# Attention and SoLU layer on one core: all four full query tiles of batches 1 to 3 turned through DRAM and VectorE instead of two

## The chip, the cores and the metric

The kernel runs on 1 core of one Trainium2 chip. The metric is device time in microseconds (us) of one launch. Before the change three timed runs took 480.44, 481.09 and 484.1 us, so the median is 481.09. The engines are called by the profile's names: PE (TensorE matmul), PEld (its weight load), DVE (VectorE), ACT (ScalarE), POOL (GpSimd) and SP (SyncE, which here only issues DMAs; its queue is SPq). Buffers in PSUM are called `pd` (two banks) and `pg` (one bank).

## What is computed

Attention over 4 batches, 8 heads, 576 positions and 64 columns a head, with rotary position embedding, is laid out as 2304 rows of 512 and goes through a layer with SoLU and a layer norm:

```python
q_rot, k_rot = (rotate(q), rotate(k))
scores = scale * np.matmul(q_rot, k_rot.transpose(0, 1, 3, 2))
scores = scores - np.max(scores, axis=-1, keepdims=True)
attn = np.exp(scores)
attn = attn / (np.sum(attn, axis=-1, keepdims=True) + 1e-09)
x = (attn @ v)            # 2304 rows of 512
h = x @ w_in              # 512 -> 1024
sm = softmax(h); solu = h * sm
ln = (solu - mean) / np.sqrt(var + 1e-06) * g_ln
out = ln @ w_out          # 1024 -> 512
```

All inputs and the output are float32.

## The kernel before

**Stages.** Two heads make a pair; there are 16 pairs, four to a batch. For each pair `stage` turns q and k by the rotary tables (L350, three VectorE or GpSimd operations for each) and, from pair 4 on, splits them into a high and a low part (`kh`, `kl`, `qh`, `ql`). `attention` then takes the 576 query rows of each head in four full tiles of 128 rows (`pair_tile`, i = 0 to 3, both heads at once) and one packed tile that holds the last 64 rows of both heads (`packed`). For a full tile PE makes the scores (L409), DVE takes the row maximum (`mx`, L389) and ACT writes the exponentials to one of four SBUF buffers `e` (L391).

**Turning.** The product with v needs the exponentials with the keys on the partitions, so each full tile and head (an (i, h), eight for a pair) is turned once; the 64 last columns and the packed tile are always turned by PE. `turn_tile` has two ways for it. By PE: four transposes against the identity `idn` (L449) into a `pg` bank, and one copy by ACT or DVE (L319, L321) out of it into `ET`. By DRAM: SP issues a write of the tile to scratch (`escr<-e`, L468, recorded as L334) and, once that has landed, a read back into the same buffer in another order (`e<-escr`, L469), and DVE turns 32 x 32 blocks from it into `ET` (L470, a STREAM_TRANSPOSE). Which (i, h) take the second way is the list `OFFS[P]`. After that come the products with v (L521), the row sums (L535 to L538, `rs`, `rscr`, `Rb`) and the scaled write to `xT` (L526).

**The dense layer.** When a batch is through attention, its tiles of 128 rows go through `front` (L591, 24 matmuls; maximum L598, exponential L600, product L602, then `uscr<-u`, a write to DRAM) and `back` (`wraw<-uscr`, a read; DVE turns it, L643; high and low parts `lnh`, `lnl`, L319 to L321 and L653; L661, 24 matmuls; L664 and L666 write `o`). They run beside the attention of the next batch. The dense layer of batch 3 has no attention beside it and stands at the end.

**Order.** Nothing is scheduled at run time. The kernel body notes every step with the steps it depends on; `ORDER` is a table of numbers in which the steps are then issued, `FLIP` says which of the steps that may run on either of two engines take the second one, and `BUFS` says which buffer of its pool each use takes. Each engine works through its own steps in that order, and so does SP's one DMA queue.

Of the kernel before, what the change touches and what calls it, by code (L numbers as in the profile page):

```python
# [28 lines left out]
OFFS = [()] * 4 + [((0, 0), (0, 1), (2, 0), (2, 1))] * 12  # L29

ORDER = [
    4, 0, 3, 11, 2, 1, 10, 12, 5, 13, 27, 14, 15, 94, 35, 28, 6, 16, 17, 18, 97, 98, 103, 95, 29, 30, 36,
    96, 31, 104, 105, 106, 7, 32, 99, 100, 37, 38, 39, 40, 107, 114, 115, 127, 128, 101, 102, 110, 111, 116,
    117, 84, 89, 33, 108, 112, 129, 113, 83, 109, 19, 118, 20, 86, 85, 87, 136, 139, 137, 121, 138, 91, 119,
    130, 131, 88, 120, 90, 92, 122, 123, 124, 125, 126, 140, 147, 148, 132, 41, 42, 149, 133, 93, 143, 155,
    178, 59, 34, 156, 144, 145, 146, 157, 158, 152, 154, 181, 153, 182, 150, 151, 134, 135, 179, 180, 159,
    170, 169, 187, 171, 141, 176, 173, 142, 172, 174, 183, 184, 60, 163, 164, 165, 188, 189, 211, 190, 191,
    196, 197, 61, 160, 62, 63, 64, 214, 215, 198, 199, 21, 177, 162, 253, 212, 213, 166, 167, 161, 168, 220,
    257, 223, 194, 195, 256, 224, 8, 9, 425, 51, 200, 221, 222, 231, 258, 22, 23, 201, 192, 193, 261, 202,
    218, 185, 232, 24, 219, 43, 186, 254, 233, 239, 240, 216, 217, 255, 229, 230, 262, 265, 263, 241, 25,  # L40
    26, 343, 242, 225, 243, 226, 227, 205, 206, 228, 342, 52, 264, 53, 54, 55, 207, 44, 208, 65, 45, 267,
    271, 268, 266, 236, 238, 260, 56, 209, 337, 237, 274, 275, 269, 272, 204, 270, 273, 295, 246, 203, 244,
    210, 57, 46, 58, 47, 48, 426, 234, 235, 427, 276, 277, 428, 429, 49, 296, 297, 75, 247, 248, 249, 250,
    298, 251, 50, 76, 278, 279, 282, 245, 283, 252, 430, 299, 77, 67, 68, 284, 285, 304, 315, 78, 79, 80,
    280, 300, 281, 301, 344, 175, 289, 290, 291, 259, 305, 306, 316, 317, 292, 293, 307, 338, 339, 69, 70,
    320, 322, 321, 340, 341, 286, 287, 288, 350, 294, 353, 351, 308, 309, 310, 323, 324, 302, 303, 318, 311,
    352, 71, 349, 319, 72, 73, 74, 312, 354, 359, 362, 360, 325, 326, 313, 314, 355, 356, 66, 363, 357, 654,
    434, 358, 383, 386, 384, 443, 444, 435, 436, 437, 438, 439, 331, 332, 333, 361, 653, 364, 385, 365, 392,
    334, 335, 345, 346, 387, 390, 440, 395, 396, 327, 330, 328, 461, 403, 391, 393, 394, 329, 336, 348, 370,
    371, 372, 373, 397, 398, 445, 446, 452, 447, 374, 448, 375, 366, 376, 81, 661, 368, 441, 648, 369, 367,  # L50
    388, 82, 453, 664, 665, 404, 662, 405, 377, 378, 462, 663, 666, 379, 380, 381, 389, 672, 431, 401, 402,
    649, 669, 650, 659, 382, 500, 406, 667, 407, 432, 501, 673, 674, 502, 503, 408, 410, 655, 411, 409, 412,
    413, 414, 415, 504, 399, 454, 675, 676, 670, 677, 696, 400, 419, 420, 421, 422, 423, 656, 678, 463, 464,
    465, 466, 470, 699, 700, 704, 683, 697, 698, 701, 660, 442, 455, 467, 468, 651, 707, 456, 457, 506, 708,
    709, 684, 710, 507, 685, 686, 347, 469, 471, 740, 668, 416, 505, 472, 473, 474, 711, 475, 681, 682, 671,
    508, 509, 519, 520, 510, 712, 713, 718, 497, 719, 657, 417, 476, 477, 705, 679, 680, 521, 418, 424, 511,
    525, 741, 526, 527, 720, 458, 528, 512, 514, 515, 723, 724, 706, 725, 658, 716, 717, 742, 687, 702, 522,
    449, 516, 726, 523, 727, 728, 479, 652, 478, 524, 529, 729, 721, 714, 715, 538, 513, 530, 753, 756, 757,
    539, 751, 690, 433, 691, 517, 692, 754, 755, 746, 693, 689, 531, 694, 703, 761, 722, 764, 767, 480, 765,
    768, 766, 688, 695, 481, 758, 482, 544, 483, 533, 545, 540, 541, 459, 542, 484, 546, 547, 485, 771, 773,  # L60
    774, 543, 769, 460, 534, 762, 763, 772, 788, 734, 486, 487, 759, 735, 736, 737, 738, 532, 557, 558, 770,
    760, 782, 783, 548, 488, 784, 785, 791, 549, 786, 489, 789, 775, 790, 730, 731, 732, 550, 776, 490, 491,
    492, 792, 493, 733, 494, 739, 495, 496, 450, 451, 551, 799, 800, 796, 777, 563, 564, 565, 802, 745, 747,
    778, 576, 580, 566, 743, 744, 801, 797, 581, 582, 748, 749, 518, 498, 803, 499, 591, 535, 779, 780, 577,
    578, 810, 811, 812, 559, 560, 579, 818, 561, 781, 819, 787, 553, 815, 816, 817, 845, 848, 846, 847, 849,
    813, 752, 814, 583, 584, 585, 594, 586, 587, 798, 595, 598, 833, 793, 794, 588, 837, 838, 839, 840, 795,
    820, 821, 589, 590, 592, 808, 809, 552, 850, 562, 804, 805, 806, 807, 856, 826, 827, 828, 829, 830, 822,
    599, 832, 834, 835, 612, 596, 597, 859, 860, 601, 554, 857, 858, 567, 568, 572, 602, 569, 571, 600, 603,
    593, 536, 537, 613, 824, 851, 825, 823, 831, 609, 853, 867, 843, 925, 842, 604, 605, 606, 607, 854, 608,
    614, 868, 852, 869, 870, 750, 616, 617, 570, 610, 611, 615, 880, 883, 865, 866, 881, 884, 882, 861, 862,  # L70
    863, 836, 891, 864, 902, 855, 874, 875, 876, 892, 893, 894, 888, 895, 555, 556, 841, 903, 937, 904, 905,
    618, 924, 926, 940, 941, 871, 877, 906, 910, 573, 844, 929, 927, 872, 873, 878, 879, 907, 909, 885, 928,
    627, 948, 938, 900, 574, 951, 949, 908, 901, 619, 889, 575, 630, 896, 897, 620, 621, 622, 623, 911, 912,
    939, 890, 634, 952, 930, 631, 886, 887, 942, 931, 932, 972, 973, 936, 913, 950, 898, 899, 974, 632, 975,
    976, 959, 624, 625, 626, 953, 628, 983, 984, 914, 985, 945, 954, 977, 986, 633, 987, 635, 980, 915, 916,
    917, 918, 919, 920, 921, 922, 923, 933, 994, 1214, 960, 961, 962, 637, 1215, 957, 638, 943, 958, 978,
    629, 981, 992, 639, 993, 636, 934, 640, 979, 995, 963, 645, 1217, 955, 1218, 1216, 944, 641, 1207, 642,
    643, 935, 1206, 1208, 982, 946, 1209, 947, 644, 1225, 1226, 956, 966, 1210, 996, 967, 1228, 968, 1229,
    1227, 969, 970, 646, 1249, 965, 964, 971, 1219, 988, 989, 1002, 997, 998, 1016, 1017, 1022, 1220, 1003,
    1250, 1251, 990, 1201, 991, 1222, 1004, 1018, 1019, 1252, 1005, 999, 1000, 1001, 1236, 1232, 1020, 1237,  # L80
    1238, 1221, 1213, 1298, 647, 1254, 1239, 1223, 1224, 1021, 1233, 1023, 1234, 1235, 1253, 1006, 1008,
    1024, 1025, 1026, 1007, 1230, 1202, 1203, 1204, 1257, 1035, 1036, 1260, 1261, 1010, 1011, 1012, 1240,
    1013, 1027, 1028, 1014, 1263, 1271, 1009, 1015, 1262, 1255, 1231, 1256, 1205, 1264, 1306, 1272, 1273,
    1212, 1243, 1244, 1245, 1246, 1247, 1309, 1241, 1310, 1294, 1293, 1295, 1299, 1029, 1300, 1242, 1276,
    1278, 1258, 1296, 1030, 1259, 1111, 1277, 1041, 1037, 1038, 1307, 1308, 1248, 1269, 1270, 1042, 1274,
    1279, 1280, 1043, 1281, 1112, 1113, 1039, 1114, 1040, 1115, 1282, 1116, 1275, 1317, 1265, 1266, 1117,
    1305, 1318, 1391, 1319, 1267, 1044, 1054, 1055, 1314, 1045, 1268, 1031, 1032, 1033, 1118, 1304, 1046,
    1050, 1301, 1302, 1119, 1283, 1047, 1287, 1285, 1311, 1288, 1289, 1386, 1290, 1291, 1049, 1315, 1320,
    1321, 1341, 1344, 1345, 1286, 1284, 1292, 1328, 1034, 1329, 1120, 1121, 1326, 1297, 1327, 1122, 1342,
    1123, 1322, 1343, 1124, 1051, 1323, 1352, 1312, 1125, 1313, 1126, 1316, 1355, 1052, 1053, 1330, 1331,  # L90
    1127, 1060, 1048, 1129, 1324, 1056, 1356, 1359, 1057, 1353, 1354, 1346, 1133, 1360, 1363, 1130, 1211,
    1325, 1335, 1336, 1337, 1338, 1339, 1364, 1365, 1332, 1390, 1392, 1347, 1348, 1333, 1371, 1372, 1334,
    1340, 1398, 1399, 1134, 1135, 1393, 1373, 1397, 1349, 1394, 1058, 1059, 1401, 1368, 1131, 1400, 1061,
    1062, 1132, 1374, 1403, 1375, 1128, 1370, 1369, 1357, 1385, 1387, 1388, 1402, 1358, 1350, 1303, 1396,
    1361, 1362, 1478, 1063, 1064, 1065, 1069, 1066, 1136, 1366, 1367, 1351, 1137, 1138, 1068, 1139, 1070,
# [754 lines left out]
```

## Time and profile before

| | before |
|---|---|
| median of 3 runs | 481.09 us |
| the profiled execution's own time | 482.13 us |
| its span, first to last instruction | 480.3 us |
| PE busy | 452.9 us (94%) |
| DVE busy | 391.0 us (81%) |
| ACT busy | 278.5 us (58%) |
| POOL busy | 175.4 us (37%) |
| DMA engines, mean busy share | 57.2% of 16 engines for SP's queue, 86.74 MB |

A busy share is the time in which the engine had an instruction in work, out of the span. Matmuls overlap, and the ends of matmuls are modelled, so PE at 94% is not PE at its peak: how close one matmul stands behind the other is read from the starts in the timeline. The span and the time differ by 1.8 us, which lies ahead of the first and behind the last instruction.

### The profile page before, as it was taken

The numbers are of one execution on the slowest core, as the hardware profiler recorded it, in microseconds if no ns is written. First come the engines' busy times: TensorE is split into PE (matmuls) and PEld (weight loads), VectorE is DVE, ScalarE is ACT, GpSimd is POOL, SyncE is SP. The second block draws the span as 40 slices with busy tenths as digits, with TensorE's granted clock in tenths as the row PEclk, the third lists the DMA queues.
The fourth block names the chain that finished last, engine by engine and source line by source line (L and its number), as shares of the span: only waits on it lengthen the run. The fifth ranks groups of instructions, "written<-read, shape, count | busy, mean of one in ns | idle before, by whom it ended". The sixth has DMA issues, their size and how long they took to land.

```text
span 480.3 us, 8209 instructions
## 1 busy us (share of the span) xinstructions
PE 452.9 (94%) x2880; PEld 330.7 (69%) x2880; DVE 391.0 (81%) x658; ACT 278.5 (58%) x622; POOL 175.4 (37%) x142
## 2 busy tenths in 40 slices
PE   1989999999999999999999999999999999999986
PEld 1555666777777666767777777686777786778865
DVE  3889999998978896879887888978778788675773
ACT  1677979887755655565745564655655555233323
POOL 1033233248367564153633252534621521011120
PEclk9999999999999999999999999999999999999999
DMA  7456565495665665757567476556756456143341
GB/s 268 164 173 226 174 214 165 130 289 180 196 186 172 222 214 183 268 143 226 195 175 239 138 240 228 151 188 201 212 189 177 151 162 194 51 145 111 127 139 64
DMA packets 63610, 87.27 MB, mean 182 GB/s; under 512 B 6080, under 2 KB 44240, under 8 KB 63568
## 3 DMA queue, kind: packets, MB, share of 16 engines
q1 hardware_dynamic: 63568, 86.74, 57.2%
q8 instruction: 23, 0.38, 0.3%
q14 instruction: 19, 0.16, 0.1%
HBM read 59.90 MB, written 26.81 MB: 181 GB/s over the span
## 4 chain that ended last, share of the span: by engine, by line
PE 69%; DVE 19%; ACT 5%; issue 3%; DMA 2%; POOL 1%; SPq 0%; DVEq 0%; ACTq 0%; POOLq 0%
PE pg L661 16%; PE pd L591 15%; PE pg L521 13%; PE pd L409 12%; PE pg L449 10%; DVE mx L389 4%; PE pd L431 2%; DVE tb L643 2%; DVE ET L470 2%; ACT e L391 1%; DVE ms L598 1%; DVE acc L535 1%; ACT u L600 1%; DMA tabs<-in_tab_dram 1%; ACT ET L319 1%
## 5 line engine op out<-in xcount | busy, mean ns | idle before, releaser
L391 ACT ACTIVATE e<-pd,mx 128x576 f32<-128x576 f32 x144 | 106.3, 741 | 63.5 <-DVE mx L389 50.2
L389 DVE TENSOR_REDUCE mx<-pd 128x1 f32<-128x576 f32 x144 | 103.5, 747 | 13.5 <-PE pd L409 11.7
L449 PE MATMUL pg<-idn,e 128*128 128x128 f32 (+1 forms) x464 | 79.1, 294 | 4.5 <-ACT rs L319 1.3
L449 PEld LDWEIGHTS pg<-idn,e 128*128 128x128 f32 (+1 forms) x464 | 63.8, 196 | 25.1 <-issue 4.7
L521 PE MATMUL pg<-ET,vst 128*64 128x320 f32 (+1 forms) x512 | 70.5, 412 | 1.2 <-ACT ET L319 0.9
L591 PE MATMUL pd<-wih,xh 128*128 128x512 f32 x144 | 61.5, 427 | 0.0
L661 PE MATMUL pg<-woh,lnh 128*128 128x512 f32 x144 | 59.5, 413 | 0.7 <-DVE lnh L321 0.7
L661 PE MATMUL pg<-woh,lnl 128*128 128x512 f32 x144 | 56.5, 392 | 1.0 <-DVE lnl L653 1.0
L591 PE MATMUL pd<-wih,xl 128*128 128x512 f32 x144 | 56.6, 393 | 0.0
L591 PE MATMUL pd<-wil,xh 128*128 128x512 f32 x144 | 56.3, 391 | 0.0
L661 PE MATMUL pg<-wol,lnh 128*128 128x512 f32 x144 | 56.2, 390 | 0.0
L470 DVE STREAM_TRANSPOSE ET<-e 128x512 f32<-128x512 f32 x48 | 53.7, 1134 | 2.4 <-DMA e<-escr 2.4
L319 ACT COPY ET<-pg 128x512 f32<-128x512 f32 x82 | 46.6, 587 | 14.1 <-PE pg L449 13.4
L521 PEld LDWEIGHTS pg<-ET,vst 128*64 128x64 f32 x512 | 34.0, 136 | 26.9 <-issue 3.2
L653 POOL TENSOR_TENSOR lnl<-tb,lnh 128x512 fp32r<-128x512 f32 x22 | 28.3, 1287 | 58.5 <-DVE lnh L321 28.3
L643 DVE STREAM_TRANSPOSE tb<-wraw 128x512 f32<-128x512 f32 x36 | 38.6, 1090 | 0.5 <-DMA wraw<-uscr 0.5
L409 PE MATMUL pd<-kh,qh 64*128 64x288 f32 x192 | 35.9, 343 | 0.3 <-ACT e L391 0.3
L409 PE MATMUL pd<-rotk,rotq 64*128 64x288 f32 x128 | 25.2, 482 | 11.1 <-DVE rotq L350 10.3
L350 POOL TENSOR_TENSOR rawk<-rawk,tabs 128x576 f32<-128x576 f32 x18 | 26.0, 1446 | 20.7 <-DMA rawk<-in_k_t_dram 20.7
L661 PEld LDWEIGHTS pg<-woh,lnh 128*128 128x128 f32 x144 | 27.2, 189 | 8.4 <-issue 1.6
L600 ACT ACTIVATE u<-pd,ms 128x1024 f32<-128x1024 f32 x18 | 20.1, 1117 | 22.0 <-DVE ms L598 15.9
L620 POOL TENSOR_TENSOR ms<-ms,half 128x1 f32<-128x1 f32 x18 | 10.4, 578 | 61.1 <-DVE ms L618 58.2
(101 smaller groups left out, 866.9 us busy)
## 6 DMA issues: line engine op xcount, KB each, us to landing
escr<-e SPq DMA_DIRECT2D x48, 256.0 KB
e<-escr SPq DMA_DIRECT2D x48, 256.0 KB
rawq<-in_q_t_dram SPq DMA_DIRECT2D x16, 576.0 KB
uscr<-u SPq DMA_DIRECT2D x18, 512.0 KB
wraw<-uscr SPq DMA_DIRECT2D x18, 512.0 KB
rawk<-in_k_t_dram SPq DMA_DIRECT2D x15, 576.0 KB
vst<-in_v_t_dram SPq DMA_DIRECT2D x16, 320.0 KB
out_dram<-o SPq DMA_DIRECT2D x18, 256.0 KB
```

Source lines behind the costliest of these rows:

```text
L319: nc.scalar.copy(o, i)
L350: add(*c[0], prio, lambda e: e.tensor_tensor(o, a, b, op=op), r, w, alt=c[1], two=True)
L389: add("dve", 672, t, lambda: nc.vector.tensor_reduce(mx[:, mcol:mcol + 1], buf(us)[:, :, 0:288], axis=AX.XY, op=ALU.max, negate=True), [sk ...
L391: add("act", 720, t, lambda: nc.scalar.activation(e.rearrange("p (z n) -> p z n", z=2), buf(us)[:, :, 0:288], AF.Exp, bias=mx[:, mcol:mcol ...
L409: nc.tensor.matmul(buf(us)[:, z, 0:288], a[rows, c0:c0 + 128], w[rows, 288 * z:288 * z + 288], start=(j == 0), stop=(j == len(terms) - 1))
L449: nc.tensor.transpose(dst, src, idn)
L470: add("dve", 1040, t, lambda: nc.vector.transpose(ET[r][:, h, :, q0:q0 + 128].rearrange("p m (a j) -> p j m a", j=4), e.rearrange("p (j b ...
L521: nc.tensor.matmul(buf(uy)[rows, 0:nq], vv[:, m, h, :], e, start=(m == 0), stop=(m == 4))
L591: nc.tensor.matmul(buf(uh)[:, z, :], a[:, c, :], w[:, c, HF * z:HF * z + HF], start=(c == 0 and j == 0), stop=(c == KC - 1 and j == 2))
L643: add("dve", 1050, tl, lambda z=z, turned=turned: nc.vector.transpose(turned().rearrange("p m (a j) -> p j m a", j=4), v[:, :, 128 * z:128 ...
L653: add(*c[0], tl, lambda e, hd=hd, ld=ld, turned=turned: e.tensor_tensor(ld, turned(), hd, op=ALU.subtract), [bk] + kl[0][z], kl[1][z], use ...
L661: nc.tensor.matmul(buf(uo), a[:, f, :], w[:, f, :], start=(f == 0 and j == 0), stop=(f == FC - 1 and j == 2))
```

## The change

`OFFS` lists all eight (i, h) for the pairs 4 to 15 where it listed the four of tiles 0 and 2. Batch 0 (pairs 0 to 3) still turns all of them by PE. With that, `ORDER`, `FLIP` and `BUFS` are other tables: there are 48 steps more (2303) and 48 uses of a buffer fewer.

```diff
-OFFS = [()] * 4 + [((0, 0), (0, 1), (2, 0), (2, 1))] * 12
+OFFS = [()] * 4 + [tuple((i, h) for i in range(4) for h in range(2))] * 12
 
 ORDER = [
...
-    4, 0, 3, 11, 2, 1, 10, 12, 5, 13, 27, 14, 15, 94, 35, 28, 6, 16, 17, 18, 97, 98, 103, 95, 29, 30, 36,
...
 FLIP = {
-    16, 34, 42, 57, 58, 73, 85, 86, 88, 89, 117, 169, 171, 172, 173, 253, 254, 255, 258, 285, 338, 339, 342,
...
+    10, 16, 17, 18, 42, 50, 58, 82, 85, 86, 88, 89, 90, 153, 158, 170, 172, 173, 174, 201, 217, 219, 254,
...
```

What this does to the engines' queues, counted over the whole of both orders: PE has 192 transposes (L449) fewer. SP has 48 writes `escr<-e` and 48 reads `e<-escr` more. DVE has 48 STREAM_TRANSPOSE (L470) more; of other work it has 10 copies `ET<-pg`, 8 casts to `lnh`, 8 subtractions for `lnl`, 4 products for `rawk`, 5 for `rawq` and 3 sums for `rotk` fewer, 2 `xh`, 2 `xl` and 4 weight casts fewer, and some half a dozen small ones either way. ACT has 38 copies `ET<-pg` fewer and 15 casts more. POOL has 13 operations more, among them the 8 for `lnl`, 9 products for `rawk` and `rawq` and 3 sums for `rotk`.

Three places show it. The first is PE in batch 2, between the packed tiles of two pairs (`wih`, `wil` are the parts of the first weights, `xh`, `xl` those of the rows). Before:

```order
L591 MATMUL pd_117<-wih,xl 128x512
L449 MATMUL pg_118<-idn,e_89 128x128 x4
L591 MATMUL pd_117<-wih,xh 128x512
L591 MATMUL pd_117<-wil,xh 128x512
L591 MATMUL pd_117<-wih,xl 128x512
L449 MATMUL pg_119<-idn,e_87 128x128 x4
L591 MATMUL pd_117<-wih,xh 128x512
```

Of the change, the same stretch shows matmuls of the dense layer between two pieces of one product with v:

```order
L538 MATMUL pg_119<-idn,acc_101 4x128
L521 MATMUL pg_119<-ET_92,vst_85 64x320 x6
L591 MATMUL pd_115<-wih,xh 128x512
...
L591 MATMUL pd_115<-wih,xl 128x512
L521 MATMUL pg_119<-ET_92,vst_85 64x320 x2
L409 MATMUL pd_117<-kh_83,qh_79 128x288
```

The groups of four transposes between the dense matmuls are gone.

The second place is DVE in the same batch (ET_91 and ET_92 are the two halves of `ET`). Before:

```order
L470 STREAM_TRANSPOSE ET_91<-e_88 128x4x4x32 x2
L389 TENSOR_REDUCE mx<-pd_116 128x1
L621 SCALAR_TENSOR_TENSOR ms<-ms 128x1
L321 COPY rs_97<-pg_118 4x128
L666 SCALAR_TENSOR_TENSOR o<-pg_119,ms,o 128x512
L389 TENSOR_REDUCE mx<-pd_115 128x1
L643 STREAM_TRANSPOSE tb<-wraw 128x4x128
L321 COPY ET_92<-pg_119 128x4x128
```

In the change:

```order
L470 STREAM_TRANSPOSE ET_91<-e_88 128x4x4x32 x2
L617 TENSOR_SCALAR ms<-ms 128x1
L618 SCALAR_TENSOR_TENSOR ms<-ms 128x1
L536 RECIPROCAL acc_100<-acc_100 128x5
L470 STREAM_TRANSPOSE ET_92<-e_89 128x4x4x32
L389 TENSOR_REDUCE mx<-pd_116 128x1
L389 TENSOR_REDUCE mx<-pd_115 128x1
L470 STREAM_TRANSPOSE ET_92<-e_89 128x4x4x32
```

The copy out of `pg` has left DVE, and further block transposes of other tiles stand between the row maxima that ACT waits for.

The third place is SP's queue in batch 2. Before:

```order
L334 DMA escr<-e_87 128x4x128
L334 DMA rscr<-rs_97 4x128
L334 DMA Rb<-rscr 64x256
L334 DMA escr<-e_87 128x4x128
L334 DMA Rb<-rscr 64x256
L334 DMA out_dram<-o 128x512
L606 DMA uscr<-u 128x4x256
L334 DMA escr<-e_90 128x4x128
```

In the change:

```order
L334 DMA escr<-e_87 128x4x128 x2
L334 DMA rscr<-rs_97 4x128
L334 DMA escr<-e_88 128x4x128
L334 DMA vst_86<-in_v_t_dram 128x640
L334 DMA e_90<-escr 128x512
L334 DMA e_87<-escr 128x512
L334 DMA escr<-e_88 128x4x128
L334 DMA e_88<-escr 128x512
L334 DMA Rb<-rscr 64x256
L334 DMA e_87<-escr 128x512
```

Writes and reads of three different buffers now stand in one another's way on the one queue, and the loads and row sums stand among them.

## Rows read from the trace of the kernel before

**Rows 1.** The page: busy time of each engine, and then some of the lines of 40 equal slices (busy tenths; PEclk is the granted TensorE clock in tenths).

```profile
PE 452.9 (94%) x2880; PEld 330.7 (69%) x2880; DVE 391.0 (81%) x658; ACT 278.5 (58%) x622; POOL 175.4 (37%) x142
...
PE   1989999999999999999999999999999999999986
...
DVE  3889999998978896879887888978778788675773
...
PEclk9999999999999999999999999999999999999999
DMA  7456565495665665757567476556756456143341
```

**Rows 2.** Busy time by stage: the attention of batch 0 (0 to 105 us), the stage in which batches 1 to 3 go through attention and batches 0 to 2 through the dense layer (105 to 408 us), and the dense layer of batch 3 (408 to 480 us). Columns: length, then for each engine busy us and instructions, granted clock, DMA share, GB/s.

```profile
0.00:105.00 105.00, 88.95 (x585) 59.12 (x587) 92.38 (x169) 76.35 (x179) 28.18 (x25) 1.00 0.60 197
105.00:408.00 303.00, 297.29 (x1990) 219.15 (x1991) 253.31 (x415) 178.74 (x403) 137.49 (x107) 1.00 0.63 195
408.00:480.00 72.00, 66.67 (x309) 52.46 (x307) 45.32 (x76) 23.43 (x41) 9.69 (x11) 1.00 0.32 106
```

**Rows 3.** The page: the chain of waits that ended last, shares of the span by engine and by line.

```profile
PE 69%; DVE 19%; ACT 5%; issue 3%; DMA 2%; POOL 1%; SPq 0%; DVEq 0%; ACTq 0%; POOLq 0%
PE pg L661 16%; PE pd L591 15%; PE pg L521 13%; PE pd L409 12%; PE pg L449 10%; DVE mx L389 4%; PE pd L431 2%; DVE tb L643 2%; DVE ET L470 2%; ACT e L391 1%; DVE ms L598 1%; DVE acc L535 1%; ACT u L600 1%; DMA tabs<-in_tab_dram 1%; ACT ET L319 1%
```

**Rows 4.** PE's timeline around one group of four transposes: start, duration, instruction.

```profile
241.59 0.39 PE L591 MATMUL pd<-wil,xh 128*128 128x512 f32 x1
241.81 0.40 PE L591 MATMUL pd<-wih,xl 128*128 128x512 f32 x1
242.05 0.64 PE L449 MATMUL pg<-idn,e 128*128 128x128 f32 x4
242.44 0.47 PE L591 MATMUL pd<-wih,xh 128*128 128x512 f32 x1
242.76 0.39 PE L591 MATMUL pd<-wil,xh 128*128 128x512 f32 x1
242.98 0.40 PE L591 MATMUL pd<-wih,xl 128*128 128x512 f32 x1
243.22 0.64 PE L449 MATMUL pg<-idn,e 128*128 128x128 f32 x4
```

**Rows 5.** Groups of instructions of the whole run, shapes kept apart: busy us and mean ns of one, then idle time of the engine just before them and what ended it.

```profile
L449 PE MATMUL pg<-idn,e 128*128 128x128 f32 x448 | 74.9, 294 | 4.5 <-ACT rs L319 1.3 <-DVE ms L617 1.1 <-DVE o L666 0.8
...
L470 DVE STREAM_TRANSPOSE ET<-e 128x512 f32<-128x512 f32 x48 | 53.7, 1134 | 2.4 <-DMA e<-escr 2.4
...
L350 DVE TENSOR_TENSOR rawq<-rawq,tabs 128x576 f32<-128x576 f32 x15 | 12.9, 870 | 0.0
...
L653 DVE TENSOR_TENSOR lnl<-tb,lnh 128x512 fp32r<-128x512 f32 x14 | 11.4, 815 | 1.4 <-ACT lnh L319 0.8
...
L350 DVE TENSOR_TENSOR rawk<-rawk,tabs 128x576 f32<-128x576 f32 x14 | 11.3, 809 | 5.4 <-DMA tabs<-in_tab_dram 5.3
...
L321 DVE COPY ET<-pg 128x512 f32<-128x512 f32 x14 | 9.5, 682 | 2.3 <-PE pg L449 2.3
...
L321 DVE CAST lnh<-tb 128x512 fp32r<-128x512 f32 x16 | 7.7, 481 | 3.0 <-PE pg L661 2.6
...
L350 DVE TENSOR_TENSOR rotk<-rawk 128x576 f32<-128x576 f32 x8 | 6.0, 751 | 0.4
...
L449 PE MATMUL pg<-idn,e 128*64 128x128 f32 x16 | 4.5, 279 | 0.0
```

**Rows 6.** DMA of the middle stage (105 to 408 us): packets, bytes and share of 16 engines of SP's queue, and the two DMAs of a turn, with count and KB of one.

```profile
q1 hardware_dynamic: 49392, 58.63, 62.5%
...
e<-escr SPq DMA_DIRECT2D x44, 256.0 KB
escr<-e SPq DMA_DIRECT2D x44, 256.0 KB
```

**Rows 7.** Busy time by stage, columns as in rows 2: the 12 us with the highest DMA share, and 72 us of batch 0.

```profile
96.00:108.00 12.00, 12.00 (x85) 8.62 (x84) 11.79 (x21) 10.35 (x22) 5.75 (x5) 1.00 0.93 289
...
36.00:108.00 72.00, 68.91 (x479) 46.46 (x476) 69.80 (x130) 60.32 (x141) 24.05 (x18) 1.00 0.63 199
```

**Rows 8.** What SP's queue waited for in the middle stage, 37 groups, longest first, with us in total, times and the longest; the last line is the last group.

```profile
SPq L334 <- DMA escr<-e: 41.2, 23, 5.4
SPq L334 <- ACT e L391: 28.6, 15, 5.2
SPq L334 <- DMA rscr<-rs: 25.2, 14, 3.3
SPq L334 <- ACT rs L319: 18.1, 11, 2.7
SPq L633 <- DMA uscr<-u: 15.9, 5, 4.5
SPq L606 <- DVE ms L617: 11.3, 4, 3.9
SPq L334 <- DVE o L666: 7.9, 3, 4.6
...
SPq L334 <- PE pd L409: 0.2, 1, 0.2
```

**Rows 9.** The two DMAs of a turn on SP's queue, whole run: ns of issue, least, median and most.

```profile
L334 SPq DMA_DIRECT2D escr<-e x48: 359/390/590, 91.1 to 405.1; - x48
L334 SPq DMA_DIRECT2D e<-escr x48: 319/336/877, 93.6 to 408.3; - x48
```

**Rows 10.** The longest group of waits on ACT in the middle stage: us in total, times, longest.

```profile
ACT e L391 <- DVE mx L389: 32.7, 27, 4.7
```

**Rows 11.** The wait of DVE for a turn's read in the middle stage, same columns.

```profile
DVE ET L470 <- DMA e<-escr: 1.6, 2, 0.8
```

More of the change, by code (lines that the diff above doesn't have):

```diff
@@ L27 @@
 SPLIT = 4
-OFFS = [()] * 4 + [((0, 0), (0, 1), (2, 0), (2, 1))] * 12
+OFFS = [()] * 4 + [tuple((i, h) for i in range(4) for h in range(2))] * 12
 ORDER = [
[121 rows of a table removed]
[124 rows of a table added]
 ]
 FLIP = {
[8 rows of a table removed]
[6 rows of a table added]
 }
 BUFS = (
-    "0101210011102001011011011200010000102111010102011010112111101010120011100002101021010112010110021010"
-    "0100100100201201211011002111110220110201102112101012120101210110202011102010000211011020000001021110"
-    "0010112122200121010112100110212112001100202101101100220000002101110100100101010102112101111000220000"
-    "1012010102011001100101021121021200120201001121211010000022000011210201010010122110000211201001001211"
-    "2000102121010210010110220211121100121010201"
+    "0100210111002011200001110121101101112010101012101110002100010010121000011012011120001010012100101100"
+    "0002011002102002111212101010212111110110021112102111100022110021211111002020100120102100100220220011"
+    "0010021020102010200001221110011101011101211211110110100021012011110120102112001011012112020200101001"
+    "20211210112101211011001000011010100112201112001121010102110121101110110021120022101210101210021"
 )
```

256 rows, old and new, of tables (FLIP, ORDER) are left out of this document.

## The prediction

> **What bounds the kernel now.** I read the page first, then the stages, then the chain of waits, and last the timeline of PE and SP's queue. The page shows one clock, full speed, in every slice, and PE and DVE as the two busy engines [rows 1]; the clock is no term here. Cut by stages [rows 2], the run falls into three. In the first 105 us (attention of batch 0) nothing is turned through DRAM, neither before nor after; DVE is busy 69.80 of 72 us there from 36 to 108 us [rows 7] and sets the pace. In the last 72 us PE works off the dense layer of batch 3. The change sits between, in the 303 us from 105 to 408 us, and there the reader is to see PE busy 297.3, DVE 253.3 and the DMA engines at 0.63 [rows 2]. So PE is the limit of that stage: a matmul starts 0.22 or 0.23 us behind the last one for long stretches [rows 4]. The chain agrees: 69% of the span on PE, of it 10% on the transposes of L449, but 19% on DVE [rows 3].
>
> **PE's term.** 192 transposes go, 48 groups of four. A group starts at 242.05 and the matmul behind it at 242.44, so it holds PE for 0.39 us; and that matmul takes 0.32 us to the next start (242.76) where a dense one takes 0.23, 0.09 us more [rows 4]. 48 x 0.48 = 23 us. The chain gives a little less: 10% of 480.3 us over the 448 + 16 transposes of L449 is 0.10 us for each, 192 of them 20 us [rows 3, 5]. I take 23: all of it lies in the middle stage and on its limit. PE's busy time there falls to 297 - 23 = 274 us.
>
> **DVE's term.** 48 block transposes at 1.134 us are +54.4 us [rows 5]. What leaves DVE, by the counts of the order: 10 copies x 0.682 = 6.8, 8 casts x 0.481 = 3.8, 8 subtractions x 0.815 = 6.5, 4 x 0.809 and 5 x 0.870 = 7.6, 3 x 0.751 = 2.3 [rows 5], and the weight casts, `xh` and `xl` less the few small ones that come to DVE, some 2: together 29. Net +25 us; counted by the position of the row maxima in both orders, about 2 of it falls in batch 0, so +23 in the middle stage: 253 + 23 = 276 us. DVE has 50 idle us there now, and these hide it only as far as they fall where it has work ready.
>
> **The DMA engines' term.** 48 writes and 48 reads of 256 KB are 25.2 MB. The middle stage moves 58.63 MB in 62.5% of 303 us, that is 189 busy us or 0.31 MB a busy us [rows 6], so the new ones add 81 us: 270 us. In the middle stage they are a resource at 0.89 of today's length, where they were at 0.63.
>
> **What else moves.** ACT loses 38 copies and gains 15 casts, and it had 303 - 179 = 124 us free [rows 2]: nothing, unless its exponentials come later for want of row maxima, for which it already waits 32.7 us [rows 10]. POOL gains 13 operations, some 20 us on 137 of 303 [rows 2]: nothing; the cover is that it runs a pair ahead. The order of batch 0 and of the tail is new, but DVE's work in the one is within 2 us of the old and the dense matmuls left after the last scores are 240 in either order: nothing from either, with 2 us each way kept.
>
> **The sum.** The stage now has three resources with nearly the same need: PE 274, DVE 276, DMA 270 us. None can be packed fully. PE today is packed to 297.3/303 = 0.98 [rows 2], with DMA at 0.63. DVE was packed to 69.8/72 = 0.97 where it led, also with DMA at 0.63 [rows 7]. All three close to full at once exists, but for 12 us: PE 12.00, DVE 11.79, DMA 0.93 [rows 7]. The upper end of the gain is DVE packed as PE is now: 276/0.98 = 282 us, 21 less. At 276/303 = 0.91 nothing is gained. I take the packing midway between 0.97, which DVE has shown with one companion, and 0.91, that is 0.94, since a third full resource has never been held for more than a few us here: 276/0.94 = 294 us, 9 less. The profiled execution took 482.13 us and becomes 473; the median of the runs lies 1.0 below it, 481.1, so the forecast for the median is **472 us**.
>
> **Rivals.**
>
> *SP's queue becomes the limit (slower).* A turn's read may only be issued when its write has landed, and SP waits for that in order with every load, row sum and output behind it. In the middle stage it waited 41.2 us for 23 of the 44 writes, 1.8 us for each wait and 0.94 for each write [rows 6, 8]. Issuing takes 0.39 + 0.34 us a turn [rows 9]. 48 more turns cost SP 35 us of issue and between 45 us (as often as now) and 86 us (a wait for each): 80 to 121 us. What they can use up is the time in which SP now waits for engines, 109 us over the groups that name one, 28.6 the longest and 0.2 the last [rows 8]; the rest of its waits are landings (41.2, 25.2 and 15.9). At 80 us SP still has room, at 121 the stage grows by 12 us, to a median of 493. It decides at (109 - 35)/48 = 1.5 us of waiting for each new turn. Against it: DVE waited for a turn's read 1.6 us in all [rows 11], and the new order issues two writes before it asks for the first read. For it: with the DMA engines at 0.9 a landing takes longer than at 0.63, and the longest wait was already 5.4 us.
> The Trainium skill, in "DMA: Bandwidth & Descriptors", section "Anatomy of one DMA", puts a fixed 2 us on a DMA, most of it until the last byte is confirmed as landed, and says that the issuing sequencer does all the waiting. Its section was fitted on another issue path than SP's; by it alone each new turn would hold SP for 2.0 us and this rival would be the forecast: 35 + 96 = 131 us, 22 over the room, a median of 503. The trace's 1.8 us for a wait comes near its figure; that only 23 of 44 writes were waited for at all is why I give it the smaller chance.
>
> *Nothing is gained.* DVE takes PE's place at once: the transposes that PE no longer does are late on DVE by as much, in front of the row maxima. DVE's packing would stay at 0.91 and the stage at 303. For it: DVE already is 19% of the chain [rows 3]. Median 481.
>
> *PE's whole term is gained.* DVE is packed to 0.98 and PE to 274/282: 21 us, a median of 460. For it are the 12 us in rows 7 alone.
>
> **How the numbers follow.** About 1% (4.8 us) is what a measurement of this kernel can tell from no change, since its three runs spread over 0.8%. My forecast, a gain of 3 to 17 us, has a chance of 0.50, of which 0.05 lies within 1%; the full gain 0.12; no gain 0.17; SP's queue 0.21, all of it beyond 1%. So faster 0.57, same 0.22, slower 0.21. The range: below, the full gain, 460 less 1 for the order of batch 0 and the tail, 459; above, SP's queue with most of its 12 us, 490. That leaves out about 0.03 below and 0.09 above.
>
> **What would show it.** In the changed profile the middle stage should be about 294 us long, with PE near 274 busy us, DVE near 276 and the DMA share near 0.9; the first and the last stage as long as now within 2 us. The chain should show PE's transposes of L449 fall from 10% to about 6% and DVE rise above 19%. ACT's wait for the row maxima should grow beyond 33 us. Wrong would be: a DMA share that stays below 0.8 with SP waiting over 90 us for `escr<-e` (then SP's queue leads), PE still above 290 busy us, or a gain that sits in the first 105 us.

## The result and the profile after

The change made the kernel faster: a median of 468.37 us (467.71 to 469.83, 4 runs) against 481.92 us (480.44 to 484.1, 4 runs) for the kernel before on the same chip. The ratio is 0.9719, with a 95% interval from 0.9672 to 0.9767, so 13.5 us are gone. Some executions of a kernel are disturbed and slower; every median here counts them and every ratio leaves them out. The profiled execution took 468.83 us, with a span of 466.9 us against 480.3.

The page of the changed kernel, busy time of each engine and three of the lines of 40 slices, beside [rows 1]:

```profile
PE 435.8 (93%) x2688; PEld 312.2 (67%) x2688; DVE 406.1 (87%) x665; ACT 266.1 (57%) x597; POOL 197.9 (42%) x160
...
PE   1999999999989999889999999989999999999996
...
DVE  3799999999999999798899989998899998586771
...
DMA  7575536698888998999997989999889896543431
```

PE has lost 17 busy us and DVE has gained 15. The line to look at is the last one: from the ninth slice to the thirty-third the DMA engines stand at 8 or 9 tenths (once at 7), where they mostly stood at 5 to 7.

Where did the time go? The block transposes of L470 mark the stage in which turns go through DRAM. One row of the trace gives their count, their shortest, median and longest duration in ns, and the start of the first and of the last. Before:

```profile
L470 DVE STREAM_TRANSPOSE ET<-e x48: 1066/1134/1196, 102.0 to 420.1; 128x512 f32<-128x512 f32 x48
```

After:

```profile
L470 DVE STREAM_TRANSPOSE ET<-e x96: 1068/1129/2280, 102.9 to 409.2; 128x512 f32<-128x512 f32 x96
```

From the first to the last it is 318.1 us before and 306.3 after: 11.8 us less. What comes behind the last one is 60.2 and 57.7 us: 2.5 less. The first starts 0.9 later. Together that is the 13.4 us by which the span is shorter.

Busy time by stage, with the columns of [rows 2]; the second cut is put at 394 us, so that 73 us remain behind it as 72 did before. It goes by the time that remains and not by the work: of the 14 us between 303 and 289 the block transposes put 11.8 into the stage and the rest behind it.

```profile
0.00:105.00 105.00, 89.63 (x574) 59.50 (x576) 92.63 (x173) 76.50 (x178) 25.64 (x23) 1.00 0.65 211
105.00:394.00 289.00, 278.31 (x1804) 199.63 (x1802) 268.26 (x417) 164.66 (x377) 155.92 (x122) 0.99 0.89 279
394.00:467.00 73.00, 67.89 (x315) 53.08 (x310) 45.22 (x76) 24.96 (x44) 16.34 (x16) 1.00 0.39 131
```

In the middle row PE is at 278 of 289 us, DVE at 268 and the DMA engines at 0.89. SP's queue moved this much there, against 58.63 MB in [rows 6]:

```profile
q1 hardware_dynamic: 77573, 80.35, 88.6%
```

The chain of waits, against [rows 3]:

```profile
PE 46%; DVE 31%; issue 8%; DMA 7%; ACT 5%; POOL 1%; SPq 1%; DVEq 0%; ACTq 0%
PE pg L661 15%; PE pd L591 11%; PE pg L521 9%; PE pd L409 8%; DVE mx L389 8%; DVE ET L470 6%; DMA e<-escr 2%; DMA escr<-e 2%; PE pg L449 2%; ACT e L391 2%; DVE tb L643 2%; DVE ms L598 2%; PE pd L431 1%; DMA tabs<-in_tab_dram 1%; DVE xT L526 1%
```

PE's share has fallen from 69% to 46%. DVE has 31%, and the two transfers of a turn, which were not in the list, have 2% each. The chain now goes to and fro between PE, DVE and the transfers.

The waits of ACT in the middle stage, total us, times and longest, against the 32.7 us of [rows 10]:

```profile
ACT e L391 <- DVE mx L389: 24.5, 21, 3.1
...
ACT e L391 <- DVE ET L470: 17.8, 10, 3.9
```

The second row was 2.2 us in the whole run before. An exponential writes into a buffer `e`, and a buffer that is turned through DRAM comes free only when DVE has turned what is in it, behind a write and a read. More of them are held so long, and ACT waits for them; whether more than four buffers would take this wait away was not tried.

SP's queue in the middle stage, against [rows 8]:

```profile
SPq L334 <- ACT e L391: 38.5, 36, 3.6
SPq L334 <- DMA escr<-e: 28.9, 24, 2.7
```

SP waited for the landing of 24 writes, 1.2 us each, where it waited 1.8 us each for 23. Summed over all groups of the stage, it waited 79 us for engines and 43 us for landings, against 109 and 84 before.

### The profile page after: what moved, and what is told of

Same layout as the page of the kernel before. It is cut to its first block, busy times and chain, and to the rows that moved or that the text cites. A ratio compares the mean times of both kernels' runs of the same rounds, so it can differ in the third digit from the quotient of the medians.

```text
span 466.9 us, 7952 instructions
## 1 busy us (share of the span) xinstructions
PE 435.8 (93%) x2688; PEld 312.2 (67%) x2688; DVE 406.1 (87%) x665; ACT 266.1 (57%) x597; POOL 197.9 (42%) x160
## 4 chain that ended last, share of the span: by engine, by line
PE 46%; DVE 31%; issue 8%; DMA 7%; ACT 5%; POOL 1%; SPq 1%; DVEq 0%; ACTq 0%
PE pg L661 15%; PE pd L591 11%; PE pg L521 9%; PE pd L409 8%; DVE mx L389 8%; DVE ET L470 6%; DMA e<-escr 2%; DMA escr<-e 2%; PE pg L449 2%; ACT e L391 2%; DVE tb L643 2%; DVE ms L598 2%; PE pd L431 1%; DMA tabs<-in_tab_dram 1%; DVE xT L526 1%
## 5 line engine op out<-in xcount | busy, mean ns | idle before, releaser
L391 ACT ACTIVATE e<-pd,mx 128x576 f32<-128x576 f32 x144 | 106.3, 741 | 81.2 <-DVE mx L389 28.9
L470 DVE STREAM_TRANSPOSE ET<-e 128x512 f32<-128x512 f32 x96 | 107.7, 1143 | 6.5 <-DMA e<-escr 6.2
L521 PE MATMUL pg<-ET,vst 128*64 128x256 f32 (+1 forms) x512 | 73.0, 419 | 2.0 <-DMA vst<-in_v_t_dram 0.9
L653 POOL TENSOR_TENSOR lnl<-tb,lnh 128x512 fp32r<-128x512 f32 x30 | 38.7, 1292 | 74.0 <-ACT lnh L319 50.1
L591 PE MATMUL pd<-wih,xh 128*128 128x512 f32 x144 | 59.6, 414 | 1.0 <-DVE xh L321 0.8
L449 PE MATMUL pg<-idn,e 128*128 128x128 f32 (+1 forms) x272 | 50.3, 300 | 6.7 <-ACT ET L319 3.0
L521 PEld LDWEIGHTS pg<-ET,vst 128*64 128x64 f32 x512 | 37.7, 138 | 27.3 <-issue 2.5
L449 PEld LDWEIGHTS pg<-idn,e 128*128 128x128 f32 (+1 forms) x272 | 37.0, 188 | 24.1 <-ACT ET L319 7.4
L350 POOL TENSOR_TENSOR rawk<-rawk,tabs 128x576 f32<-128x576 f32 x22 | 31.4, 1431 | 9.1 <-DMA tabs<-in_tab_dram 5.9
L350 POOL TENSOR_TENSOR xl<-xT,xh 128x512 fp32r<-128x512 f32 x14 | 18.0, 1288 | 37.1 <-ACT xh L319 20.0
L591 PEld LDWEIGHTS pd<-wih,xh 128*128 128x128 f32 x144 | 27.3, 190 | 8.7 <-issue 2.4
```

The costliest lines, as they stand in the source:

```text
L350: add(*c[0], prio, lambda e: e.tensor_tensor(o, a, b, op=op), r, w, alt=c[1], two=True)
L391: add("act", 720, t, lambda: nc.scalar.activation(e.rearrange("p (z n) -> p z n", z=2), buf(us)[:, :, 0:288], AF.Exp, bias=mx[:, mcol:mcol ...
L449: nc.tensor.transpose(dst, src, idn)
L470: add("dve", 1040, t, lambda: nc.vector.transpose(ET[r][:, h, :, q0:q0 + 128].rearrange("p m (a j) -> p j m a", j=4), e.rearrange("p (j b ...
L521: nc.tensor.matmul(buf(uy)[rows, 0:nq], vv[:, m, h, :], e, start=(m == 0), stop=(m == 4))
L591: nc.tensor.matmul(buf(uh)[:, z, :], a[:, c, :], w[:, c, HF * z:HF * z + HF], start=(c == 0 and j == 0), stop=(c == KC - 1 and j == 2))
```

## The experiments

Four questions: is PE still the limit, is it DVE, is it the transfers or the queue that issues them, and is the gain one of the turns or of the order they stand in? My theory was that three resources set the pace by turns, so that relief of one pays little and of several more. The rivals are that one alone leads, and that the order alone made the gain. Each ratio is to the kernel before on the same chip; where I give us, it is the difference of two ratios times 481.9.

### PE's term alone, in the kernel before

```diff
-return [(bt[:, 128 * m:128 * m + 128], chunk(ej[:, base:base + 512], m)) for m in range(4)]
+return [(bt[:, 128 * m:128 * m + 128], chunk(ej[:, base:base + 512], m)) for m in range(1 if P >= 4 else 4)]
```

> The kernel before, in its own order, with one transpose instead of four in each of the 48 groups that the change takes off PE (three quarters of those tiles are left out, the copy out of PSUM stays). It shows PE's term alone, without anything new on DVE or the DMA engines: 144 transposes at about 0.10 us are 14 us. If PE set the pace of the middle stage before, as forecast, 8 to 14 us less than before (467 to 473). If DVE set it as much as PE (19% of the chain), under 5 us less.

Measured: 475.17 us, ratio 0.9868 [0.9794, 0.9942], 6 us faster. PE's busy time over the run fell from 452.9 to 441.2 us, so about half of it came out at the end. The stage, cut at 400 us:

```profile
105.00:400.00 295.00, 286.22 (x1859) 203.81 (x1859) 251.55 (x417) 179.34 (x407) 137.52 (x107) 1.00 0.65 201
```

Neither DVE nor the DMA engines got any more work, and still PE's packing (its busy time over the length of the stage) fell from 0.98 to 286.22/295 = 0.97, and DVE rose from 19% to 21% of the chain. Half of PE's term is lost without any new load. That other engines, in their fixed order, could not come that much earlier would fit; which of them it was, the run does not show. It bears on the change too: in the old order three quarters of PE's relief, with nothing added, gave 6 us, and the change gave 13.5 with more work for DVE and the DMA engines. So its new order probably has a part in the gain.

### Less work for PE, in the kernel after

```diff
 for j, (a, w) in enumerate(((xh, wih), (xh, wil), (xl, wih))):
+    if j == 1 and i < 13:
+        continue
```

> The changed kernel without one of the three matmuls (low part of the first weights) for the dense tiles of batches 0 to 2: 13 tiles x 8 x 0.23 us = 24 us less PE work in the middle stage, all else alike. If PE still sets the pace of that stage: 15 to 24 us below the changed kernel's 468. If DVE does: 0 to 4 us below. If PE, DVE and the DMA engines hold each other up by turns (my theory): 4 to 10 us below.

Measured: 467.54 us, ratio 0.9709 [0.9634, 0.9784]: nothing that the intervals tell from the changed kernel, where my theory had 4 to 10 us. The stage, cut at 391 us, and the chain:

```profile
105.00:391.00 286.00, 260.92 (x1698) 180.43 (x1696) 266.07 (x416) 162.77 (x373) 155.21 (x122) 1.00 0.91 283
```

```profile
DVE 33%; PE 30%; DMA 17%; issue 9%; ACT 7%; SPq 4%; DVEq 0%; ACTq 0%
```

PE has 17 busy us less in the stage, and even in the profiled execution, the fastest of its four, the stage is only 3 us shorter (286 against 289). So behind the change, in this order, PE alone no longer sets the pace, though the page shows it 93% busy.

### Less work for DVE, less for the transfers, and both

First, half the columns in 48 of the block transposes:

```diff
+nj = 2 if i % 2 else 4
...
-    ET[r][:, h, :, q0:q0 + 128].rearrange("p m (a j) -> p j m a", j=4),
+    ET[r][:, h, :, q0:q0 + 128].rearrange("p m (a j) -> p j m a", j=4)[:, 0:nj],
```

> The changed kernel with block transposes of half the columns for the tiles 1 and 3 (the other half of their exponentials is left as it was): 48 x 0.57 us = 27 us less DVE work, all else alike. If DVE alone sets the pace of the middle stage now: 18 to 27 us below 468. If PE does: 0 to 4 us. By my theory of three resources by turns, with DVE the one with most in the chain: 6 to 14 us below.

Measured: 467.42 us, ratio 0.9679 [0.9609, 0.9748]: 2 us, which the intervals don't tell from none; my theory had 6 to 14. DVE's busy time in the stage, cut at 389 us, fell by 21 us.

Then half the data in the same 48 turns, with as many DMAs as now:

```diff
-dma(t, sc.rearrange("i p c -> p i c"), e.rearrange("p (i c) -> p i c", i=4), 0, [ke], [ks], xf=728.0)
+ni = 2 if i % 2 else 4
+dma(t, sc[0:ni].rearrange("i p c -> p i c"), e[:, 0:128 * ni].rearrange("p (i c) -> p i c", i=ni), 0, [ke], [ks], xf=728.0)
```

> The changed kernel with writes and reads of half the data in the turns of tiles 1 and 3 (the other half is not moved): 12.6 MB less, at the 0.31 MB a busy us of the changed middle stage 40 us less for the DMA engines, with as many DMAs on SP's queue as before. If the DMA engines set the pace at a share of 0.89: 15 to 30 us below 468. If SP's order does: 0 to 5 us. By my theory: 3 to 10 us below.

Measured: 462.23 us, ratio 0.9589 [0.953, 0.9648]: 6 us faster than the changed kernel. In the stage, cut at 388 us, the DMA share fell to 0.80, 31 busy us less, with DVE (266 us) and PE (275 us) nearly as busy as before. Each transfer is also shorter: SP waited 14.9 us for landings of writes instead of 28.9. So the run does not tell the load of the DMA engines from the length of a single turn.

And both cuts together:

> The changed kernel with half the data in the turns of tiles 1 and 3 and block transposes of half the columns for them, the two cuts of the earlier runs together (27 us less on DVE, 40 us less on the DMA engines). Alone they gave 1 and 6 us. If the two hold each other up by turns: 10 to 18 us below 468, more than the sum. If the DMA engines alone set the pace: 5 to 7 us below.

Measured: 458.75 us, ratio 0.9483 [0.9451, 0.9515]: 11 us faster than the changed kernel, and 5 us faster than with less data alone, which the intervals tell apart. The 11 are 3 more than 2 and 6, but the four intervals together leave some 5 us either way: that the two pay more together than apart is not shown.

The groups of the block transposes show how DVE and the reads hang together. Columns: count, busy us, mean ns; then the idle time of DVE just before them and how much of it a turn's read ended. The changed kernel:

```profile
L470 DVE STREAM_TRANSPOSE ET<-e 128x512 f32<-128x512 f32 x96 | 107.7, 1143 | 6.5 <-DMA e<-escr 6.2
```

With less work for DVE:

```profile
L471 DVE STREAM_TRANSPOSE ET<-e 128x512 f32<-128x512 f32 (+1 forms) x96 | 84.1, 896 | 10.5 <-DMA e<-escr 10.4
```

With less data:

```profile
L471 DVE STREAM_TRANSPOSE ET<-e 128x512 f32<-128x512 f32 x96 | 106.1, 1133 | 0.4 <-DMA e<-escr 0.2
```

With both:

```profile
L472 DVE STREAM_TRANSPOSE ET<-e 128x512 f32<-128x512 f32 (+1 forms) x96 | 83.2, 892 | 1.9 <-DMA e<-escr 1.9
```

A quicker DVE waits longer for the reads (10.4 us instead of 6.2); smaller transfers take this wait away (0.2). With both cuts DVE is quicker and waits 1.9 us. But most of the 21 us went elsewhere. These are the waits of DVE's row maxima for PE's scores in the stage (us in total, times, longest), in the changed kernel, with less work for DVE, and with both cuts (the stage cut at 394, 389 and 384 us):

```profile
DVE mx L389 <- PE pd L409: 1.7, 7, 0.4
DVE mx L389 <- PE pd L409: 9.5, 14, 1.9
DVE mx L389 <- PE pd L409: 12.9, 16, 1.8
```

A quicker DVE waits 4 us more for reads and 8 us more for scores. With both cuts the chain stands on PE again:

```profile
PE 62%; DVE 19%; issue 7%; ACT 5%; DMA 5%; SPq 0%; POOL 0%; DVEq 0%; ACTq 0%
```

### All three cuts

> The changed kernel with all three cuts at once: two of three matmuls with the first weights for the dense tiles of batches 0 to 2 (24 us less PE), half the columns in the block transposes (27 us less DVE) and half the data (40 us less DMA) for tiles 1 and 3. PE's cut alone gave 1 us, DVE's 1, the DMA engines' 6, the last two together 10. If three resources hold each other up by turns, PE is next once the other two have room: 5 to 12 us below the run with two cuts (447 to 454). If PE no longer matters: within 2 us of its 459.

Measured: 455.26 us, ratio 0.9457 [0.9425, 0.9488]: 1 us beyond the two cuts, with intervals that overlap, where my theory had 5 to 12. The two runs come from different chips; by their medians alone it would be 3.5 us. The stage, cut at 379 us, and the chain:

```profile
105.00:379.00 274.00, 256.18 (x1688) 177.44 (x1690) 246.98 (x414) 161.00 (x372) 153.92 (x121) 1.00 0.82 251
```

```profile
PE 45%; DVE 27%; DMA 9%; issue 8%; ACT 7%; SPq 2%; POOL 0%; DVEq 0%; ACTq 0%
```

PE is at 0.93 of the stage, DVE at 0.90 and the DMA engines at 0.82, and 16 busy us less for PE than with two cuts (272 to 256) still pay next to nothing, though the chain with two cuts stood at 62% on PE: a share of the chain is not what relief pays. My theory expected PE to be next when the other two are relieved; that part of it fell. No resource is full here. What holds the stage then must be waits between queues whose fixed order was made for other durations; this last sentence is argued from the rows, no run shows it by itself.

Taken together, my theory foretold the cut of data and the two cuts, and missed the cuts of PE, of DVE and of all three. What the runs show is a rank: relief of the transfers pays alone (6 us), relief of DVE only beside it (5 us), relief of PE next to nothing.

### The same work in the other order

The changed kernel's turns in the old order: the steps that both kernels have stand as they did, each new write, read and block transpose was put in by hand.

```diff
 ORDER = [
-    2, 4, 1, 3, 5, 19, 6, 10, 11, 12, 13, 27, 14, 15, 17, 16, 18, 84, 20, 94, 97, 98, 35, 83, 21, 22, 7, 95,
+    4, 0, 3, 11, 2, 1, 10, 12, 5, 13, 27, 14, 15, 94, 35, 28, 6, 16, 17, 18, 97, 98, 103, 95, 29, 30, 36,
...
```

> All eight turned through DRAM and the engines chosen as in the changed kernel, but every step that both kernels have is issued in the order of the kernel before; the 48 new turns stand in the places of the transposes and copies that they replace, with their write and read moved ahead (28 and 64 steps ahead of the block transpose at most). If the gain is the turn itself and the order only fits it in: 466 to 472. If a good part of the gain is the new order (my theory since the PE term alone gave 6 us of 14): 474 to 484, with waits of DVE for reads or of ACT for free buffers.

Measured: 612.33 us, ratio 1.2542 [1.2477, 1.2607]. The work is the same as after the change and takes 136 us more, far beyond either expectation. Its waits over the whole run:

```profile
ACT e L391 <- DVE mx L389: 100.5, 55, 8.9
...
DVE ET L470 <- DMA e<-escr: 40.6, 20, 5.7
```

DVE stands in front of a read that has not landed, the row maxima stand behind it, and ACT waits for those.

And the old turns in the new order, with tiles 1 and 3 back on PE:

```diff
-OFFS = [()] * 4 + [tuple((i, h) for i in range(4) for h in range(2))] * 12
+OFFS = [()] * 4 + [((0, 0), (0, 1), (2, 0), (2, 1))] * 12
```

> The reverse: tiles 1 and 3 turned by PE again as before, every step that both kernels have issued in the order and on the engines of the changed kernel, the transposes at the place of the read and the copy, by ACT, behind them. PE has its 23 us back, DVE 54 us less, the DMA engines 81 us less. If the gain is the turn: 476 to 484. If the gain is the order and the choice of engines: 466 to 473.

Measured: 522.95 us, ratio 1.0808 [1.0767, 1.085], again far beyond either expectation. The wait on top:

```profile
ACT ET L317 <- PE pg L447: 80.7, 52, 5.0
```

ACT stands in front of each copy out of `pg` until PE has come to the four transposes. Both kernels are slower than either of the two whose order was made for them, so neither run prices the turns or the order apart from the other; they show that an order fits one set of steps. A milder one puts back one turn in eight:

```diff
-OFFS = [()] * 4 + [tuple((i, h) for i in range(4) for h in range(2))] * 12
+OFFS = [()] * 4 + [tuple((i, h) for i in range(4) for h in range(2))[:7]] * 12
```

> The changed kernel with one of the eight turns of a pair (tile 3, second head) back on PE and ACT, 12 in all, at the place of its read: the DMA engines 20 us less, DVE 14 us less, PE 6 us more. If the DMA engines and DVE set the pace by turns: 464 to 468. If each turn needs its own place in the order, as the run with all 48 back (523) says: 1 us more for each, 474 to 482.

Measured: 475.09 us, ratio 0.9833 [0.9779, 0.9887], 5 to 6 us slower than the changed kernel: 12 turns by PE in an order made without them cost some two fifths of the gain. How much a fresh order would give the kernel before, with its own turns, was not tried. So how the 13.5 us split between the turns and the order stays open.

### Other engines and the other queue

33 casts and copies of the middle stage from DVE to ACT:

```diff
 FLIP = {
...
-    255, 258, 270, 337, 338, 339, 343, 346, 451, 460, 500, 579, 614, 648, 649, 650, 652, 653, 654, 729, 733,
+    255, 258, 270, 337, 338, 339, 343, 346, 451, 460, 579, 648, 649, 650, 652, 653, 654, 745, 749, 1033,
...
```

> The changed kernel with 33 casts and copies of the middle stage moved from DVE to ACT (same place in the order): DVE 13 us less, ACT some 17 us more of the 124 it has free. If DVE sets the pace: 458 to 464. If it does not, as the run with 27 us less of block transposes says: 466 to 470, and more if ACT's exponentials come later.

Measured: 468.89 us, ratio 0.969 [0.9644, 0.9736]: nothing that the intervals tell from the changed kernel. DVE's busy time over the run fell by 9 us (406.1 to 396.8), and its wait for the reads rose from 6.2 to 11.0 us, as in the run with less work for DVE.

The 96 writes from ACT's queue instead of SP's, in the same place of the order:

```diff
-dma(t, sc.rearrange("i p c -> p i c"), e.rearrange("p (i c) -> p i c", i=4), 0, [ke], [ks], xf=728.0)
+add("sp", 500, t, lambda: nc.scalar.dma_start(sc.rearrange("i p c -> p i c"), e.rearrange("p (i c) -> p i c", i=4)), [ke], [ks], xfer=728.0)
```

> The changed kernel with the 96 writes of a turn issued from ACT's queue instead of SP's, at the same place in the order; the amount of data and everything else alike. SP loses 96 issues (36 us) and its 39 us of waits for exponentials in the middle stage. If the one in-order queue of SP holds the changed kernel back: 458 to 465. If it is the amount of data on the DMA engines, as the run with half the data but as many DMAs (6 us less) says: 466 to 471, since ACT now issues 96 DMAs and waits where one of the eight landing counters is not free.

Measured: 473.66 us, ratio 0.9784 [0.9723, 0.9846], 3 us slower by ratio, with intervals that overlap. SP no longer waits for exponentials before a write, but it waits for the landings instead, because the reads are still its own; in the stage, cut at 398 us, 46 times and 2.0 us each:

```profile
SPq L334 <- DMA escr<-e: 92.6, 46, 6.7
```

And the same with each write right behind its exponential:

> As the run before it, with each write issued by ACT right behind the exponential that makes its data, some nine steps earlier in the order. If late writes are what DVE's 6 us of waits for reads and ACT's 18 us of waits for free buffers come from: 2 to 6 us below the run before it. If the DMA engines at a share of 0.89 are: the same within 2 us, the data queue in the engines instead.

Measured: 478.7 us, ratio 0.9917 [0.9884, 0.995], 10 us slower than the changed kernel and 6 slower than the run before it, where a gain or no change was expected. No stage is read from its profile. A second queue thus brought no gain; whether ACT's issuing cost what SP was spared is not told apart.

No version that does all of the work was clearly faster than the changed kernel.

## Why the prediction was right, point by point

The forecast was 472 us in a range of 459 to 490, faster by more than 1%; the time is 468.37. Of the 13.5 us, 11.8 lie in the middle stage, where it put 9, and 2.5 behind it, where it put 0 with 2 either way. The new order had no term of its own in the forecast; by the run with PE's term alone it probably has a part in the 13.5, and no run prices it.

**PE's term.** Forecast -23 us, to 274 in the stage. Measured: 19 less in the stage (278), and over the run 452.9 to 435.8, 17 less. The 192 transposes are gone as counted; 1.8 of the 4 us that are missing in the stage is PE's lower clock (below), the rest is not told apart. That only part of the term comes out at the end was forecast as a lower packing, and the run with PE's term alone shows it without any other load.

**DVE's term, the one that was mis-sized.** "Net +25 us" over the run was +15 (391.0 to 406.1), and 268 us in the stage instead of 276. The durations were right: count times mean, summed over all groups of DVE kept apart by form, rose from 428.9 to 458.3 us, 29.4 more, with 55.3 more for L470. But a busy time is no sum of durations: consecutive instructions of DVE overlap, by 38 us in all before and 52 after. The timeline of the changed kernel, DVE's start and duration:

```profile
343.59 1.15 DVE L470 STREAM_TRANSPOSE ET<-e 128x512 f32<-128x512 f32 x1
...
344.99 1.12 DVE L470 STREAM_TRANSPOSE ET<-e 128x512 f32<-128x512 f32 x1
346.00 1.39 DVE L389 TENSOR_REDUCE mx<-pd 128x1 f32<-128x576 f32 x2
347.30 1.12 DVE L470 STREAM_TRANSPOSE ET<-e 128x512 f32<-128x512 f32 x1
```

The block transpose at 344.99 lasts 1.12 us, and the row maximum behind it starts at 346.00, 1.01 us later. With the block transposes left out, the starts and durations in the trace give DVE 343.6 busy us before and 311.7 after. So the 48 add 47 us and not 54, and the work that left is 32 us and not 29. The Trainium skill, "Perfetto Trace Analysis", section "Optimizing Scalar/DVE Operations", gives a DVE operation an access overhead of about 60 ns on SBUF and 125 ns on PSUM, and says that a profile shows about twice this, since the write-acknowledgement half overlaps with the next instruction. The trace comes near it: the overlap is 58 ns an instruction before and 78 after on average, and 0.10 us (median) behind a block transpose of the changed kernel.

**The DMA engines' term.** Forecast 270 busy us and a share near 0.9; measured 88.6% of the 289 us, which is 256 busy us, for 80.35 MB where 58.63 + 25.2 were forecast. So this need too came out smaller, by 14 us, at the forecast 0.31 MB a busy us. Its relief is the only one that paid alone: 6 us for half the data of half the turns.

**What was put at nothing.** ACT (165 of 289 us) and POOL (156) stayed far from full, as forecast. POOL has 18 instructions more in the trace (142 to 160), where 13 operations were counted, and 18 busy us more in the stage.

**The packing.** 0.94 of the fullest resource was taken, the middle between two values, and put on DVE. DVE has 268.26/289 = 0.93, but the fullest is PE with 278.31/289 = 0.96. DVE's need as it came out, at 0.94, would have made 285 us; the stage took 289. A need that was 8 us too large and a packing that was a little too high partly cancelled. That is luck, and so is a part of the nearness of 472 to 468: with three needs of nearly one size the stage comes out nearly the same whichever is taken to lead. That three near-equal needs are packed below 0.98 held. That DVE leads them was not shown: relief of DVE alone paid 2 us, that of the transfers 6.

**What would show it.** Three full resources in the middle stage: yes. The first stage as before: 0.9 us later at the first block transpose. L449 in the chain: forecast 6%, measured 2%; DVE above 19%: 31%. Wrong was that ACT's wait for the row maxima grows beyond 33 us: it fell to 24.5. A price of the turns stands in another row, the wait for a free buffer `e`, 17.8 us; I had not asked how long a turn holds its buffer.

**The rivals.** SP's queue did not become the limit: waits of 1.2 us on average, and only for 24 of the 86 writes in the stage, with the DMA engines at 0.89, and 79 us of waits for engines still left. The Trainium skill, "DMA: Bandwidth & Descriptors", section "Anatomy of one DMA", gives a DMA on the gpsimd path a fixed cost of about 2 us, most of it until the last byte is confirmed as landed, and says that a wait for a semaphore happens on the issuing sequencer. On SP's path here 1.2 us on average and 2.7 at most of a write's landing was left to wait for. The order puts other issues between a write and its read, so this is what remains of a landing and not its length. "Nothing is gained" and "PE's whole term is gained" missed on either side; 460 us was passed only by the kernels that leave out data and DVE's work (458.75 and 455.26).

## What to carry to other kernels

When work is moved from the busiest resource to two others that come out nearly as full, only a part of the first one's relief comes out: here 13.5 us of 23, with an order made anew, which no run prices by itself. Count the transfers as one of the resources. Size a term by the distance from start to start where the trace has the operation in a row, not by its duration. In a program with a fixed order, taking load off one resource mostly turned into waits for the others, so a run that cuts one load says whether that one leads in that order, and an edit without an order of its own (the runs with 612 and 523 us) does not price the edit. Neither a busy share (PE at 93%) nor a share of the chain (PE at 62% with two cuts) says what relief will pay.

## What the runs showed that I had not expected

**PE's clock fell to half during work.** Windows of 1 us of the changed kernel, columns as in [rows 2]:

```profile
309.00:310.00 1.00, 0.43 (x4) 0.14 (x3) 1.00 (x2) 1.00 (x3) 1.00 (x2) 1.00 0.96 175
310.00:311.00 1.00, 0.44 (x2) 0.20 (x2) 1.00 (x2) 0.83 (x2) 1.00 (x1) 1.00 0.63 214
311.00:312.00 1.00, 0.53 (x5) 0.44 (x7) 1.00 (x3) 1.00 (x4) 1.00 (x2) 1.00 0.98 366
...
313.00:314.00 1.00, 1.00 (x6) 0.70 (x4) 1.00 (x2) 0.60 (x1) 0.84 (x1) 0.55 0.98 258
314.00:315.00 1.00, 1.00 (x6) 0.77 (x4) 1.00 (x3) 0.27 (x3) 0.00 (x0) 0.50 1.02 332
```

PE was busy 0.43 to 0.53 of three windows, then worked in full again, and a microsecond later the granted clock is 0.50, 1.2 instead of 2.4 GHz, until 316.5. What PE did before, from its timeline:

```profile
310.46 0.44 PE L449 MATMUL pg<-idn,e 128*128 128x128 f32 x2 [1.03 <-ACT ET L319]
311.47 0.67 PE L409 MATMUL pd<-kh,qh 64*128 64x288 f32 x2 [0.56 <-ACT e L391]
...
312.73 4.14 PE L521 MATMUL pg<-ET,vst 128*64 128x320 f32 x16
```

The longest gap is 1.03 us. The last row, a product with v at the lower clock, takes 4.14 us. In the kernel before the same sixteen matmuls take 2.37:

```profile
185.43 2.37 PE L521 MATMUL pg<-ET,vst 128*64 128x320 f32 x16
```

So this one fall made these matmuls 1.8 us longer; whether any of it reached the kernel's time is not shown, since 17 us less work for PE gave nothing either. The profiled execution of the kernel before ran at full clock up to its last instruction, and the changed turns in the old order, where PE waits most, had a mean granted clock of 0.906. But a PE that is less busy is not enough for a fall: the runs with less work for DVE and with less data have one in the same stretch of the work (at 308.2 and 308.4 us), the run with less work for PE (PE busy 90%) has none in its stage.

**SP waited less for a landing at a fuller load.** The waits of SP for a write were 1.8 us each with the DMA engines at 0.63 and 1.2 us each at 0.89. Since other issues stand between a write and its read, these are what is left of landings and not their lengths; whether a landing takes longer at the fuller load, as the forecast held, is not shown.
